# A fused memory-attention and expert kernel: sums as eight small products, a maximum in pieces, the last tile in halves, and other numbers in the planner

## The chip, the cores and the metric

The kernel runs on one core of one Trainium2 chip. The metric is the device time of one execution in microseconds. Engines go by short names: PE is TensorE (PEld its weight loads), DVE VectorE, ACT ScalarE, POOL GpSimd, SP SyncE, which issues most of the DMAs.

## The reference

Two parts follow each other. First, attention with 32 memory slots in place of 576 keys, for 8 batches and 8 heads of 64 columns:

```python
a = exp(phi - max(phi, axis=2)); a = a / (sum(a, axis=2) + 1e-9)   # over the 576 rows
k_m = einsum('bhsm,bhsd->bhmd', a, k); v_m = einsum('bhsm,bhsd->bhmd', a, v)
scores = softmax(scale * q @ k_m^T)                                # over 32 slots
x = scores @ v_m                                                   # 4608 rows of 512
```

Then a mixture of 8 experts, of which each row takes the best one:

```python
logits = x @ w_gate + modality_bias[modality_id]; e = argmax(logits)
gate = softmax(logits)[e]
out = gate * (relu(x @ w1[e]) @ w2[e])                             # 512 -> 1024 -> 512
```

## The kernel before, in words

**The work.** The kernel guesses early which expert is taken by all rows, computes with that one's weights alone and looks at the end (`bad_i`) whether the guess held. Since x is scores times v_m, the first expert product is made over the memory slots: `value_products` (L732, "vw") multiplies v_m by w1, so that a hidden tile is scores (128 slots of 4 heads, in two groups) times vw. Each big product is made of three fp32r products, high by high, low by high and high by low; the high half is a cast on ACT, the low half (`xal`, `xbl`, `vwl`, `hl`) a subtraction on DVE.

**The stages of a batch.** The maximum of phi over its rows (`mem_max`, L294 to L298: a fold of four operations on DVE; for the first batch two reductions, L306), small corrections on POOL and DVE, exp, the sums (POOL), the kv products (L403: 72 products with 32-column weights that use a quarter of the array's columns and half of its rows) and behind them one full-array product with the tile `sides` that adds the sums up over rows (L408); the turns of k_m and v_m (L148); scores ("s", L548), their softmax over slots on DVE (L593 to L625), the split of x into `xa` (part 0) and `xb` (part 1); vw twice (columns 0 to 511 and 512 to 1023, each leaving two PSUM banks that `vwl` L754 or L154 frees); the gate's small product ("vg", L528, copied by L533) and the logits ("l", L679), from which the gates come.

**The expert stages.** `hidden` (L779) makes one of 8 hidden tiles of a part: 6 products of 256 columns for part 0, 320 for part 1. ACT makes `hh` (L792) and DVE `hl` (L796) of it. `outputs` (L816) makes an output tile, 128 rows by 512 columns, in 8 steps of 3 products of 512 columns; ACT scales it by the gate (L829) and SP stores it (L837). A batch has four such tiles; a fifth (t None) takes the rest of a pair of batches. The last one of the program is that of batches 6 and 7.

**Banks.** Hidden tiles, output tiles and vw take turns in a ring of four PSUM banks ("pe"). A tile may only begin when ACT and DVE are done with the bank that is four turns back. Scores, logits, kv and vg use two other pairs of banks.

**What sets the order.** The program writes its order itself. `weave` merges two lists, the attention stages, sorted by a due time in units of expert work, and the expert stages. It keeps a model of when each engine is free, with the durations in the table `TAKES`. A stage with work for DVE is put in only if DVE's queue, by that model, is no more than a hold ahead of now: 3.5, or for the next expert stage of kind h0, h1 or h3 the number in `HOLD`. `EARLIER` moves all of a batch's due times, `AHEAD` says how far ahead of its use a batch begins. `BUSY` is the number of idle products at the start (small ones, L166, and big ones, L159); `nothing(n)` adds n more among the first stages.

## Time and profile before

| | us |
|---|---|
| median of three runs | 389.88 (389.74, 389.88, 390.06) |
| profiled execution | 389.69 |
| its span, first to last instruction | 387.9 |
| PE busy | 375.3 |
| DVE busy | 244.7 |
| ACT busy | 141.3 |
| POOL busy | 45.8 |

The span is 1.8 us shorter than the execution's time. The granted clock of TensorE is 0.994 of full speed on the mean of the span. A row of the order of time is start, duration, engine, line, operation, output<-inputs, shapes, count, and in brackets the idle time ahead with what ended it. PE records overlap: a product of 512 columns lasts 0.39 but the next starts 0.23 after it.

### The profile page before, as it was taken

The page shows a single profiled execution, that of the slowest core. Times are in us where ns is not written, and L with a number is a line of the kernel's source. Part 1 is how long each engine was busy: PE and PEld are TensorE (multiplying, and loading weights), DVE is VectorE, ACT ScalarE, POOL GpSimd, SP SyncE. Part 2 cuts the span into 40 slices and gives each one's busy share as a digit, 9 for nine tenths or more (in the row PEclk, how much of TensorE's full clock was granted, in tenths as well). Part 3 has the DMA queues.
Part 4 walks back from the last instruction along what each step waited for, and adds up shares of the span by engine and source line. Part 5 has one row for each costly group of instructions (what it writes and reads, how often), then busy time and mean ns, then how long its engine had stood idle before and what let it go on. Part 6 is the DMA issues. An engine that isn't in the chain of part 4 may idle for free.

```text
span 387.9 us, 9645 instructions
## 1 busy us (share of the span) xinstructions
PE 375.3 (97%) x3891; PEld 303.3 (78%) x3893; DVE 244.7 (63%) x613; ACT 141.3 (36%) x327; POOL 45.8 (12%) x116
## 2 busy tenths in 40 slices
PE   6899999999999999999999999999999999999993
PEld 3577976889779886788879887798868878698982
DVE  4787756895786389836786476864887467750400
ACT  2382524425234243433433334323443325241410
POOL 4347030023000400030000300003000200000000
PEclk9999999999999999999999999999999999999997
DMA  8998679875761397639712397614411011531111
GB/s 300 379 394 183 103 140 344 225 210 150 243 120 42 94 298 184 208 82 276 119 34 56 75 300 126 255 28 119 182 29 42 15 30 27 198 102 32 28 36 55
DMA packets 91307, 56.89 MB, mean 147 GB/s; under 512 B 69236, under 2 KB 74356, under 8 KB 91252
## 3 DMA queue, kind: packets, MB, share of 16 engines
q1 hardware_dynamic: 90976, 55.87, 51.4%
q8 instruction: 33, 0.54, 0.6%
q10 hardware_dynamic: 276, 0.30, 0.2%
q14 instruction: 22, 0.18, 0.2%
HBM read 37.28 MB, written 18.87 MB: 145 GB/s over the span
## 4 chain that ended last, share of the span: by engine, by line
PE 85%; DVE 4%; SPq 4%; DMA 3%; ACT 1%; issue 1%; ACTq 0%
PE pe L816 47%; PE pe L779 24%; PE pair L403 4%; PE pe L732 3%; DMA q_sb<-in_q_dram 3%; SPq L195 3%; PE pair L548 2%; PE pair L679 1%; SPq L178 1%; DVE vwl L154 1%; PE pair L148 1%; PE pair L732 1%; PE pair L408 1%; DVE xbl L662 0%; ACT ob L829 0%
## 5 line engine op out<-in xcount | busy, mean ns | idle before, releaser
L816 PE MATMUL pe<-w2h,hh 128*128 128x512 f32 x288 | 116.3, 404 | 0.0
L816 PE MATMUL pe<-w2h,hl 128*128 128x512 f32 x288 | 112.4, 390 | 0.0
L816 PE MATMUL pe<-w2l,hh 128*128 128x512 f32 x288 | 110.3, 391 | 0.0
L796 DVE SCALAR_TENSOR_TENSOR hl<-pe,hh 128x256 fp32r<-128x256 f32 (+2 forms) x158 | 58.3, 392 | 43.1 <-ACT hh L792 42.3
L816 PEld LDWEIGHTS pe<-w2h,hh 128*128 128x128 f32 x288 | 54.1, 188 | 19.8 <-issue 9.7
L792 ACT ACTIVATE hh<-pe 128x256 fp32r<-128x256 f32 (+2 forms) x158 | 53.4, 362 | 41.6 <-PE pe L779 41.2
L816 PEld LDWEIGHTS pe<-w2l,hh 128*128 128x128 f32 x288 | 54.0, 188 | 11.8
L816 PEld LDWEIGHTS pe<-w2h,hl 128*128 128x128 f32 x288 | 54.2, 188 | 9.6
L829 ACT ACTIVATE ob<-pe,gates 128x512 f32<-128x512 f32 x36 | 24.6, 687 | 73.4 <-PE pe L816 48.1
L779 PE MATMUL pe<-xbh,vwh 128*128 128x320 f32 x128 | 40.3, 315 | 0.1
L779 PE MATMUL pe<-xbh,vwl 128*128 128x320 f32 x128 | 39.6, 309 | 0.0
L779 PE MATMUL pe<-xbl,vwh 128*128 128x320 f32 x128 | 39.6, 309 | 0.0
L779 PE MATMUL pe<-xah,vwh 128*128 128x256 f32 x124 | 35.2, 287 | 1.5 <-DVE hl L796 0.7
L779 PE MATMUL pe<-xal,vwh 128*128 128x256 f32 x124 | 35.0, 284 | 0.3 <-DVE xal L662 0.3
L779 PE MATMUL pe<-xah,vwl 128*128 128x256 f32 x124 | 34.9, 283 | 0.0
L337 POOL COPY ts<-tm 32x4 f32<-32x4 f32 x24 | 4.8, 199 | 198.8 <-DVE tm L329 198.1
L779 PEld LDWEIGHTS pe<-xah,vwh 128*128 128x128 f32 x124 | 23.6, 191 | 4.2 <-ACT xah L648 1.6
L779 PEld LDWEIGHTS pe<-xbh,vwh 128*128 128x128 f32 x128 | 24.0, 188 | 1.7 <-issue 0.9
L779 PEld LDWEIGHTS pe<-xbl,vwh 128*128 128x128 f32 x128 | 24.1, 188 | 0.3
L779 PEld LDWEIGHTS pe<-xal,vwh 128*128 128x128 f32 x124 | 23.7, 191 | 0.8 <-DVE xal L662 0.5
L779 PEld LDWEIGHTS pe<-xbh,vwl 128*128 128x128 f32 x128 | 24.0, 188 | 0.0
L779 PEld LDWEIGHTS pe<-xah,vwl 128*128 128x128 f32 x124 | 23.7, 191 | 0.0
(173 smaller groups left out, 430.0 us busy)
## 6 DMA issues: line engine op xcount, KB each, us to landing
kv_sb<-in_k_dram SPq DMA_DIRECT2D x8, 1152.0 KB, 7.2
kv_sb<-in_v_dram SPq DMA_DIRECT2D x8, 1152.0 KB, 9.7
out_dram<-ob SPq DMA_DIRECT2D x64, 128.0 KB, 2.4
q_sb<-in_q_dram SPq DMA_DIRECT2D x112, 72.0 KB, 2.8
ph<-in_phi_dram SPq DMA_DIRECT2D x7, 576.0 KB, 4.3
raw<-in_moe_w_dram SPq DMA_DIRECT2D x2, 1024.0 KB, 6.4
raw<-in_moe_w_dram SPq DMA_DIRECT2D x1, 1280.0 KB, 10.2
out_dram<-ob SPq DMA_DIRECT2D x4, 256.0 KB, 2.1
```

The costliest lines, as they stand in the source:

```text
L148: nc.tensor.transpose(dst, src, ident[:rows, :rows])
L154: nc.vector.tensor_tensor(l, src, h.bitcast(F32), op=ALU.subtract)
L195: nc.sync.dma_start(*later.pop(0))
L337: nc.gpsimd.tensor_copy(ts_[BL * a:BL * (a + 1)], live["tm"][BL * o:BL * (o + 1)])
L403: nc.tensor.matmul(live["kvp"][M * j:M * (j + 1), g], lhsT=pe[half, j, c * M:(c + 1) * M], rhs=kv_sb[half, :, j, c * D:(c + 1) * D], start ...
L548: nc.tensor.matmul(sc[g][M * j:M * (j + 1), a, 0:QC * BL], lhsT=kvT[b][rows, 0, M * j:M * (j + 1)], rhs=qT[rows, j, a], start=True, stop=T ...
L732: nc.tensor.matmul(pvs[g][M * j:M * (j + 1), :], lhsT=vT[b][rows, j, :], rhs=raw1[rows, j, cols], start=True, stop=not more, tile_position ...
L779: nc.tensor.matmul(ph[:, 0:n], lhsT=(vl if k == 2 else vh)[:, g, cols], rhs=xl if k == 1 else xh, start=(g == k == 0), stop=(g == NG - 1 a ...
L792: nc.scalar.activation(hs[0][:, f, h0:h0 + p1 - p0], live["ph", f][:, p0:p1], AF.Relu)
L796: nc.vector.scalar_tensor_tensor(hl, live["ph", f][:, p0:p1], 0.0, hh.bitcast(F32), op0=ALU.max, op1=ALU.subtract)
L816: nc.tensor.matmul(po, lhsT=tile_columns(hl if n == 1 else hh, f, t), rhs=(w2l if n == 2 else w2h)[:, f, :], start=(f == n == 0), stop=(f ...
L829: nc.scalar.activation(ob, po, AF.Copy, scale=gate_of(b, t))
```

## The change

Six edits come together.

- `BUSY` goes from 92 small and 10 big idle products to 84 and 15; three `nothing` lines with 1, 4 and 3 products further on go.
- The tile `sides` and its product go. The sums are added by 8 products of 64 rows by 32 columns with a column of ones, beside each other on the array like the kv products.
- The second batch's maximum is taken by `heads_max` in three pieces (heads 0 and 1 of a partition group together, then 2, then 3), put among the first batch's stages, instead of the fold. Batches 2 to 7 keep the fold.
- The last output tile is scaled in two halves of 256 columns, one on ACT, one on DVE, and stored by two queues, SP's and ACT's.
- `HOLD` goes from 1.9, 2.4 and 2.2 to 2.2, 2.7 and 2.7.
- `EARLIER` no longer moves batch 3 (−4.0) but batch 7 (−6.0). A batch's start is its usual place minus this number, so the old value began batch 3 four later than the others, and the new one begins batch 7 six later.

```diff
--- before.py
+++ after.py
@@ -76,7 +76,7 @@
     HW = MAIN + 2 * QP
     SCALE = 1.0 / float(D) ** 0.5
     EPS = 1e-9
-    BUSY = 92, 10
+    BUSY = 84, 15
 
     FAR = float(1 << 20)
 
...
@@ -298,13 +297,16 @@
         eng.tensor_tensor(r, r, src[:, :, 8 * M:9 * M], op=op)
         return r
 
+    def heads_max(b, js):
+
+        if js.start == 0:
+            live["top", b] = wk.tile([P, HG, M], F32, name="top")
+        src = phs[b].rearrange("p j (c m) -> p j m c", m=M)
+        nc.vector.tensor_reduce(live["top", b][:, js], src[:, js], axis=AX.X, op=ALU.max)
+
     def first_max():
-
-        top = wk.tile([P, HG, M], F32, name="top")
-        src = phs[0].rearrange("p j (c m) -> p j m c", m=M)
         for js in (slice(0, HG // 2), slice(HG // 2, HG)):
-            nc.vector.tensor_reduce(top[:, js], src[:, js], axis=AX.X, op=ALU.max)
-        live["top", 0] = top
+            heads_max(0, js)
 
     def mem_max(b):
         live["top", b] = fold(nc.vector, phs[b % 2], ALU.max, "top", "top")
@@ -394,7 +396,7 @@
 
         pe, sums = live["pe", b]
         pk = pair_of_banks(1)
-        live["psum"] = pk[:, 0, 2 * D:2 * D + NG]
+        live["psum"] = pk[:, :, 2 * D]
         live["kvp"] = pk[:, :, 0:2 * D].rearrange("p g (t d) -> p g t d", t=2)
         for c in range(QC):
             for j in range(HG):
@@ -405,7 +407,13 @@
                         rhs=kv_sb[half, :, j, c * D:(c + 1) * D],
                         start=(c == 0), stop=(c == QC - 1), tile_position=(QP * g, M * j),
                     )
-        nc.tensor.matmul(live["psum"], lhsT=sums.rearrange("p j m -> p (j m)"), rhs=sides, start=True, stop=True)
+        for j in range(HG):
+            for g in range(NG):
+                half = slice(QP * g, QP * (g + 1))
+                nc.tensor.matmul(
+                    pk[M * j:M * (j + 1), g, 2 * D:2 * D + 1], lhsT=sums[half, j], rhs=ones_c[half],
+                    start=True, stop=True, tile_position=(QP * g, M * j),
+                )
 
     def first_products(t):
 
@@ -831,6 +839,15 @@
 
     def store(b, t):
         def finish(po):
+            if b == B - 1 and t is None:
+                rows = out[S * (b - 1):S * (b + 1)].rearrange("(p c) d -> c p d", c=QC)[QC - 1]
+                first, second = slice(0, DM // 2), slice(DM // 2, DM)
+                obs = [wk.tile([P, DM], F32, name="ob", bufs=2)[:, 0:DM // 2] for _ in range(2)]
+                nc.scalar.activation(obs[0], po[:, first], AF.Copy, scale=gate_of(b, t))
+                nc.vector.tensor_scalar(obs[1], po[:, second], gate_of(b, t), None, op0=ALU.mult)
+                nc.sync.dma_start(rows[:, first], obs[0])
+                nc.scalar.dma_start(rows[:, second], obs[1])
+                return
             ob = gated(b, t, po)
             if t is None:
                 rows = out[S * (b - 1):S * (b + 1)].rearrange("(p c) d -> c p d", c=QC)
@@ -862,8 +879,8 @@
...
-        "vwp": (1.15, ""), "vwpu": (1.25, "A1.1"), "vwu": (0.0, "A1.15"), "vwl": (0.0, "D1.35"),
-        "h0a": (0.24, ""), "h0b": (0.25, "A0.42 D0.45"), "k0": (2.0, ""), "kn0": (0.25, "D0.5 A0.55"), "ko0": (0.0, "D0.45"), "v0": (1.9, ""), "vn0": (0.0, "A0.5"), "kv": (2.6, "D0.4 A0.7"),
+        "vwp": (1.15, ""), "m1": (0.0, "D0.55"), "m2": (0.0, "D1.1"), "vwpu": (1.25, "A1.1"), "vwu": (0.0, "A1.15"), "vwl": (0.0, "D1.35"),
+        "h0a": (0.24, ""), "h0b": (0.25, "A0.42 D0.45"), "k0": (2.0, ""), "kn0": (0.25, "D0.5 A0.55"), "ko0": (0.0, "D0.45"), "v0": (1.9, ""), "vn0": (0.0, "A0.5"), "kv": (2.5, "D0.4 A0.7"),
...
@@ -895,7 +912,7 @@
             ("top", [("swap", b)], mem_peak, 2.0),
         ))
         for name, after, what, late in (
-            ("max", [], mem_max, 0.0),
+            *((("max", [], mem_max, 0.0),) if b > 1 else ()),
             *peaks,
             ("exp0" if b < 2 else "exp", [(peaks[-1][0], b)], mem_exp, 3.0),
             ("sums", [("exp0" if b < 2 else "exp", b)], mem_sums, 3.2),
@@ -942,9 +959,7 @@
         add(("top", 0), "top0", [("max", 0)], mem_top, 0)
         add(("preferred",), "guess", [], preferred)
         add(("guess",), "guess", [], guess)
-        nothing(1)
         add(("exp", 0), "first exp", [("top", 0)], mem_exp, 0)
-        nothing(4)
         add(("known",), "nothing", [], spread_row)
         add(("sums", 0), "first sums", [("exp", 0)], mem_sums, 0)
         add(("k", 0), "k0", [("exp", 0)], first_products, 0, floor=9.0)
@@ -986,7 +1001,6 @@
         some_hidden("hc", "h0c", [("vwl", 0, 0, 0)], range(2, 3), range(1))
         add(("vwu", 0, 1, 0), "vw1", [("vw", 0, 1)], value_upper, 1, range(1))
         add(("n", 0, 0, 1, 1), "n2", [], first_weights, 1, 1)
-        nothing(3, "pe")
         add(("xu", 0, 0, 1), "xu1", [("n", 0, 0, 1, 1)], first_split, 1, 0)
         add(("vwu", 0, 1), "vw1", [("vw", 0, 1)], value_upper, 1, range(1, 2))
         add(("w2", 0), "w2", [], first_w2, 0)
@@ -997,6 +1011,7 @@
         add(("start",), "start", [], lambda: None, floor=25.0)
         turns(1, 0, 26.5)
         turns(1, 1, 27.2)
+        add(("max", 1, 0), "m2", [], heads_max, 1, slice(0, 2), floor=26.5)
         add(("s", 0, 1), "s1", [("qt", 0, 1, 1), ("vwl", 0, 1)], first_scores, RA, RB, floor=28.6)
 
     def plan_steps(b, dues):
@@ -1049,6 +1064,11 @@
             add(("others", pair), "others", [("g", b)], others, pair)
             if b < B - 1:
                 add(("bias", pair + 1), "nothing", [], biases, pair + 1)
+        if b == 0:
+            names = [x[0] for x in todo]
+            for j, before in ((3, ("x", 0, 1)), (2, ("n", 0, 1, 0))):
+                todo.insert(names.index(before), (("max", 1, j - 1), "m1", [], heads_max, (1, slice(j, j + 1))))
+            todo += [(("max", 1), "nothing", [("max", 1, 2)], lambda: None, ())]
         for (name, kind, after, what, args), due in zip(todo, dues):
             stage(attention, name, kind, after, what, *args, due=due)
         if b == B - 1:
@@ -1113,7 +1133,7 @@
     def evenly(first, gap, n=24):
         return [first + gap * k for k in range(n)]
 
-    AHEAD, EARLIER, SPREAD = (5.8, 5.0), {3: -4.0}, 0.55
+    AHEAD, EARLIER, SPREAD = (5.8, 5.0), {7: -6.0}, 0.55
     plan_first()
     plan_steps(0, evenly(1.4, 0.25))
     plan_memory(1, 5.9, floor=27.5)
@@ -1135,7 +1155,7 @@
         at, ex = list(attention), list(experts)
 
 
-        HOLD = {"h0": 1.9, "h1": 2.4, "h3": 2.2}
+        HOLD = {"h0": 2.2, "h1": 2.7, "h3": 2.7}
 
         def ready(s):
             if not s or any(n not in done for n in s[0][2]):
...
```

The numbers set the order, so here is what is written on two engines at three places. Line numbers of the changed program are 8 or 9 higher behind L400.

DVE, batch 1, from the split of `xa` to the first hidden tiles; before:

```order
L662 TENSOR_TENSOR xal<-aT,xah 128x512
L593 STREAM_TRANSPOSE a<-pair_1084 128x320
L593 STREAM_TRANSPOSE a<-pair_1085 128x320
L754 TENSOR_TENSOR vwl<-pe,vwh 128x512 x2
L796 SCALAR_TENSOR_TENSOR hl<-pe,hh 128x256 x2
L533 COPY vg_88<-pair_1202 128x2x8
L796 SCALAR_TENSOR_TENSOR hl<-pe,hh 128x256 x2
L597 TENSOR_REDUCE mx<-a 128x20
L796 SCALAR_TENSOR_TENSOR hl<-pe,hh 128x256 x3
L599 TENSOR_TENSOR a<-a,mx 128x640
L796 SCALAR_TENSOR_TENSOR hl<-pe,hh 128x256
```

and after the change:

```order
L670 TENSOR_TENSOR xal<-aT,xah 128x512
L601 STREAM_TRANSPOSE a<-pair_1053 128x320
L601 STREAM_TRANSPOSE a<-pair_1054 128x320
L541 COPY vg_87<-pair_1170 128x2x8
L605 TENSOR_REDUCE mx<-a 128x20
L607 TENSOR_TENSOR a<-a,mx 128x640
L762 TENSOR_TENSOR vwl<-pe,vwh 128x512 x2
L804 SCALAR_TENSOR_TENSOR hl<-pe,hh 128x256 x6
```

The copy of vg, the maximum and the subtraction of the second scores (`mx`, `a`) now stand ahead of `vwl`, which stood ahead of them.

PE, batch 5, the logits and the vw product among output steps; before:

```order
L816 MATMUL pe<-w2h,hh 128x512
L816 MATMUL pe<-w2h,hl 128x512
L816 MATMUL pe<-w2l,hh 128x512
L679 MATMUL pair_3367<-aT,vg_90 32x128 x8
L679 MATMUL pair_3367<-aT,vg_90 32x32 x8
L732 MATMUL pe<-raw_106,kvT_85 32x512 x8
L816 MATMUL pe<-w2h,hh 128x512
L816 MATMUL pe<-w2h,hl 128x512
```

and now:

```order
L687 MATMUL pair_3372<-aT,vg_89 32x128 x8
L687 MATMUL pair_3372<-aT,vg_89 32x32 x8
L824 MATMUL pe<-w2h,hh 128x512
L824 MATMUL pe<-w2h,hl 128x512
L824 MATMUL pe<-w2l,hh 128x512
L824 MATMUL pe<-w2h,hh 128x512
L824 MATMUL pe<-w2h,hl 128x512
L824 MATMUL pe<-w2l,hh 128x512
L824 MATMUL pe<-w2h,hh 128x512
L824 MATMUL pe<-w2h,hl 128x512
L824 MATMUL pe<-w2l,hh 128x512
L740 MATMUL pe<-raw_105,kvT_84 32x512 x8
```

The two sets of small products followed each other; now nine products of 512 columns lie between them.

DVE, from the second scores of batch 3 to the first `hl` of the next hidden tiles, with the logits (`lgT`, `lg`), the gates (`gates`, `badp`) and batch 4's maximum (`t2top`, `top`). Before, both pairs of `vwl` stood ahead of the logits, and from the gates on the rows were:

```order
L706 TENSOR_REDUCE se<-ex 128x5
L707 TENSOR_SCALAR se<-se 128x5
L708 RECIPROCAL gates<-se 128x5
L713 TENSOR_SCALAR other<-fms,known 128x9
L714 TENSOR_REDUCE badp<-other 128x1
L294 TENSOR_TENSOR t2top<-ph_104 128x512
L295 TENSOR_TENSOR t2top<-t2top 128x4x64
L297 TENSOR_TENSOR top<-t2top 128x128
L298 TENSOR_TENSOR top<-top,ph_104 128x128
L796 SCALAR_TENSOR_TENSOR hl<-pe,hh 128x256 x4
```

Now one pair of `vwl` stands ahead of the logits and one behind the gates:

```order
L715 TENSOR_SCALAR se<-se 128x5
L716 RECIPROCAL gates<-se 128x5
L721 TENSOR_SCALAR other<-fms,known 128x9
L722 TENSOR_REDUCE badp<-other 128x1
L153 TENSOR_TENSOR vwl<-pe,vwh 128x512 x2
L293 TENSOR_TENSOR t2top<-ph_103 128x512
L294 TENSOR_TENSOR t2top<-t2top 128x4x64
L296 TENSOR_TENSOR top<-t2top 128x128
L297 TENSOR_TENSOR top<-top,ph_103 128x128
L804 SCALAR_TENSOR_TENSOR hl<-pe,hh 128x256
L329 STREAM_TRANSPOSE tt<-top 128x128
L331 TENSOR_REDUCE tm<-tt 128x4
```

The logits and gates have moved ahead of the second vw's remainder, and the maximum stays behind it, still ahead of `hl`.

4 lines of the change are left out of this document (removed).

## The prediction

> **What bounds the kernel now.** I read the page first, then a table of busy time by stretches, then the order of time around each gap.
>
> ```profile
> PE 375.3 (97%) x3891; PEld 303.3 (78%) x3893; DVE 244.7 (63%) x613; ACT 141.3 (36%) x327; POOL 45.8 (12%) x116
> PE 85%; DVE 4%; SPq 4%; DMA 3%; ACT 1%; issue 1%; ACTq 0%
> ```
>
> The first row is busy time by engine, the second the chain that ended last: TensorE (PE) is 97% busy and 85% of the chain. The table by stretches says where the missing 3% is.
>
> ```profile
> sum 25.00, PE 20.53 PEld 12.82 DVE 16.96 ACT 10.59 POOL 7.85; mean PE 4.11 PEld 2.56 DVE 3.39 ACT 2.12 POOL 1.57
> ...
> core 0: us, PE busy (x) PEld busy (x) DVE busy (x) ACT busy (x) POOL busy (x), PEclk, DMA share, GB/s
> ...
> 60.00:70.00 10.00, 9.21 (x92) 6.02 (x77) 8.22 (x17) 4.37 (x8) 0.00 (x0) 1.00 1.00 327
> ...
> 160.00:165.00 5.00, 4.26 (x36) 4.05 (x35) 4.72 (x17) 2.49 (x7) 0.29 (x2) 1.00 0.57 192
> 165.00:380.00 215.00, 215.00 (x1999) 176.71 (x1999) 124.79 (x315) 74.65 (x177) 15.25 (x34) 1.00 0.36 100
> ```
>
> PE idles 4.47 us before 25 us, then 0.79 us in the stretch from 60 to 70 and 0.74 in the one from 160 to 165. Between 165 and 380 there is no gap at all. The other stretches up to 380 are as full, and behind 380 PE has little left to do: the last tile leaves. So after 25 us an edit can pay in three ways: fill those two gaps, shorten what PE itself does, or shorten the tail. Work moved on another engine pays nothing unless PE waits for it.
>
> **The change, part by part.** The sum is made against the profiled execution, 389.69 us, which is 0.19 under the median 389.88.
>
> *Start.* Five big idle products that stood behind the first maximum move ahead of it; three at about 22 us go, with eight small ones and four memsets.
>
> ```profile
> 3.12 2.60 PE L159 MATMUL pair<-busy 128*128 128x512 bf16 x8 [0.22 <-issue]
> 6.77 0.30 PE L148 MATMUL pair<-ident,top 128*128 128x128 f32 x1 [1.05 <-DVE top L306]
> ```
>
> Eight idle products take 2.60 us and PE then waits 1.05 us for the maximum. Five more at the warm pace (half of the mean 0.33 at least, so 0.8 to 1.1 us) fill that wait; the three at 22 us stand ahead of a tile whose split ScalarE delivers later, so PE waits there with or without them. I take 0, with −0.1 to +0.3 as bounds.
>
> *The second batch's maximum.* A fold of four operations (1.6 us) goes and three pieces come.
>
> ```profile
> L306 DVE TENSOR_REDUCE top<-ph 128x64 f32<-128x576 f32 x2 | 2.2, 1118 | 4.5 <-DMA ph<-in_phi_dram 4.5
> 31.15 0.91 DVE L593 STREAM_TRANSPOSE a<-pair 128x320 f32<-128x320 f32 x2 [1.85 <-PE pair L566]
> ```
>
> The big piece costs 1.12 us and the two small ones half of that each, an estimate from the same row: 2.24 together. VectorE's idle 1.85 here takes the big one, and later gaps of the same chain, in which VectorE waits for ScalarE, the small ones. PE waits for VectorE at none of these places: 0. Without the later gaps the overhang is 2.24 − 1.85 = 0.4 of VectorE's time, and that is the bound.
>
> *Near 68 us, batch 1's first hidden tiles.* PE waited 0.46 + 0.34 = 0.80 for the split of xa; now the steps of batch 1 come earlier and the split is ready, so 0.80 is saved. But the order on VectorE at this place is a new one.
>
> ```profile
> 67.65 0.39 PE L779 MATMUL pe<-xah,vwh 128*128 128x256 f32 x1 [0.46 <-ACT xah L659]
> 68.38 0.39 PE L779 MATMUL pe<-xal,vwh 128*128 128x256 f32 x1 [0.34 <-DVE xal L662]
> ...
> 69.88 0.26 PE L528 MATMUL pair<-wgd,kvT 128*32 128x16 f32 x8
> 70.06 0.39 PE L779 MATMUL pe<-xah,vwh 128*128 128x256 f32 x1
> ...
> 298.63 5.75 PE pe L779 x48
> ...
> 69.07 1.25 DVE L754 TENSOR_TENSOR vwl<-pe,vwh 128x512 fp32r<-128x512 f32 x2
> ...
> 70.91 0.16 DVE L533 COPY vg<-pair 128x16 f32<-128x16 f32 x1
> 72.62 0.81 DVE L597 TENSOR_REDUCE mx<-a 128x20 f32<-128x640 f32 x1
> ```
>
> Before, vwl (the remainder that frees the two PSUM banks of vw) ran first, and the copy of vg, mx and the subtraction came after it, between the hl. Now vg's products stand right behind vw's, and the queue is copy, mx, subtraction, vwl. Let S be the start of vg's products on PE. They end at S+0.26, the copy at S+0.4, mx and the subtraction over the same 128x640, 0.81 each, at S+2.0, and the first half of vwl at S+2.7, when its bank is free. On PE vg takes 0.18 (69.88 to 70.06), then two tiles of six products at 0.12 each (48 in 5.75, the row of the chain), with 0.1 more at the first: PE asks for the third bank at S+1.7. It waits 1.0 us, where before it did not. Net +0.20; the bounds are −0.80 (no wait at all) and +0.6 (a second wait like it, 0.4).
>
> *Near 163 us, batch 4's first hidden tiles.*
>
> ```profile
> 160.88 0.68 DVE L294 TENSOR_TENSOR t2top<-ph 128x512 f32<-128x512 f32 x1
> ...
> 162.59 1.41 DVE L796 SCALAR_TENSOR_TENSOR hl<-pe,hh 128x256 fp32r<-128x256 f32 x4
> ...
> 163.06 0.39 PE L779 MATMUL pe<-xah,vwh 128*128 128x256 f32 x1 [0.74 <-DVE hl L796]
> ```
>
> Logits, gates and batch 4's maximum stood in one row ahead of hl, and PE waited 0.74 for the bank that hl frees. Logits and gates now come before the second vw product, six output steps earlier, so behind vwl (1.3) only the maximum (1.7, 160.88 to 162.59) is left ahead of hl. Both end before the ring is full again. I take −0.74; the other bound is 0.
>
> *Batch 3's chain four us earlier, batch 7's six us later.* Batch 3's maximum now also stands ahead of hl, of which PE needs the first one only four tiles later: 0, with little to spare. For batch 7 I have the present slack:
>
> ```profile
> 342.29 0.42 DVE L796 SCALAR_TENSOR_TENSOR hl<-pe,hh 128x256 fp32r<-128x256 f32 x1 [0.67 <-ACT hh L792]
> ```
>
> VectorE is done 0.67 us before the first hl. The later chain uses up most of this; I take 0, with 0 to +0.5 (a chain one microsecond too long for the slack would leave 0.3 to 0.5 of it on PE); beyond that it is case D below.
>
> *The eight small products.* Seven times (batches 1 to 7) one full-array product, two passes, becomes eight small ones, 16 passes.
>
> ```profile
> 365.13 16.34 PE pe L816 x72
> ...
> 173.77 0.30 PEld L408 LDWEIGHTS pair<-sides,sums 128*128 128x128 f32 x2 [0.20 <-issue]
> ...
> 174.02 0.48 PE L816 MATMUL pe<-w2h,hh 128*128 128x512 f32 x1
> 174.33 0.40 PE L816 MATMUL pe<-w2h,hl 128*128 128x512 f32 x1
> ...
> 11.51 0.29 PE L433 MATMUL pair<-ones_c,sums 64*64 64x1 f32 x8
> 11.65 2.07 PE L422 MATMUL pe<-kv_sb,exp 64*64 64x128 f32 x68
> ...
> L528 PE MATMUL pair<-wgd,kvT 128*32 128x16 f32 x64 | 2.0, 193 | 0.0
> ```
>
> Before: the weight load waits 0.20 for the small products to leave, 0.25 passes to the next big product, and the second big one comes 0.31 later instead of 0.23 (72 of them in 16.34 in the chain): 0.53 in all. After: eight small passes of L528 last 0.26 with 0.193 for the last, so they start (0.26−0.19)/7 = 10 ns apart; 15 such steps are 0.15, going in is about 0.05, and a visit of small products costs 0.21 on its way out (the last of the eight at 69.88 starts at 69.95, the next big product at 70.06, and another 0.10 is lost ahead of the one behind, as at 198.90 below). That makes 0.41, a gain of 0.12 each, 0.85 for seven. By the slowest reading of L433, 0.14 over eight passes or 17.5 ns, the eight products cost 0.53 and the gain is nothing; bounds −1.0 to 0.
>
> The Trainium skill, "TensorE: Matmul & The Clock Gate", section "Wait — 56ns, not 53.3ns?", says that matmuls never start less than about 25 ns apart however small they are; sixteen passes would then take 0.38 and the seven places would cost 0.8 more than before. The row of L433 disagrees: its eight passes, on different parts of the array, are 17.5 ns apart or less.
>
> *Visits that are no longer joined.* The higher holds on VectorE move small products on PE too: vw and logits of a batch, which ran one behind the other, are now split by output steps.
>
> ```profile
> 197.56 0.39 PE L816 MATMUL pe<-w2l,hh 128*128 128x512 f32 x1
> 197.88 1.09 PE L732 MATMUL pe<-raw,kvT 64*32 64x512 f32 x16
> 198.90 0.50 PE L816 MATMUL pe<-w2h,hh 128*128 128x512 f32 x1
> 199.24 0.39 PE L816 MATMUL pe<-w2h,hl 128*128 128x512 f32 x1
> ...
> 246.01 0.77 PE L679 MATMUL pair<-aT,vg 128*32 128x128 f32 x32
> 246.71 1.09 PE L732 MATMUL pe<-raw,kvT 64*32 64x512 f32 x16
> 247.73 0.50 PE L816 MATMUL pe<-w2h,hh 128*128 128x512 f32 x1
> ```
>
> A visit of small products costs (0.32−0.23) + (0.34−0.23) = 0.20 at its two borders, beside the 1.02 of its own; joined, the 0.70 of the logits and the 1.02 follow each other with no border. Nine pairs were joined before: vg with vw four times, logits with vw three times, scores with vw twice. Three are now, all of vg with vw. So six borders are new: four of the kinds quoted, 4 × 0.20 = 0.80, and the two with scores, which the trace shows only joined, for which I take +0.10 together out of −0.2 to +0.4. That is +0.90, with +0.6 to +1.2.
>
> *Tail.*
>
> ```profile
> L792 ACT ACTIVATE hh<-pe 128x256 fp32r<-128x256 f32 x94 | 36.1, 385 | 29.6 <-PE pe L779 29.3
> ...
> 381.54 0.69 ACT L829 ACTIVATE ob<-pe,gates 128x512 f32<-128x512 f32 x1 [4.75 <-PE pe L816]
> ...
> 0.73 0.48 ACTq L1204 DMA_DIRECT2D ph<-in_phi_dram  x1
> ```
>
> A half takes ScalarE 0.39 instead of 0.69: −0.30; VectorE's half runs beside it. The second transfer is issued by ScalarE's own queue, 0.48 for an issue, after VectorE's half; SP issued the whole one before. For that I charge 0.10 and take −0.20. The bounds are −0.35 (half the bytes in each transfer land a little sooner) and +0.1 (most of the 0.48 stands on the path).
>
> **Sum:** 0 + 0 + 0.20 − 0.74 + 0 − 0.85 + 0.90 − 0.20 = −0.69. The profiled execution comes to 389.0 and the median to 389.88 − 0.69 = 389.2.
>
> **Rivals.** *B, the prices that I charge don't fall due:* either the 1.0 us wait at batch 1 isn't there, because what VectorE does ahead of vwl is ready early, or borders cost less. For it: in the trace the vg copy, mx and the subtraction were spread among hl without delaying PE. Against it: the queue on VectorE runs in the written order. Either one gives 389.2 − 1.0 = 388.2.
>
> *C, the sums bring nothing:* the 17.5 ns above; 389.2 + 0.85 = 390.0. The full-array product is then no worse than eight small ones. For it speaks that L433's passes are the only ones with one column; against it L528's 10 ns. Should the passes be dearer still, as products that follow each other on the same part of the array might, it would be C2: 0.11 lost at each place and not won, 389.2 + 0.85 + 0.8 = 390.85. (The page's rule above is this case.)
>
> *D, slower:* batch 7's chain, six us later, ends too late. Its place lies in the stretch from 165 to 380, where PE has no gap today. PE would wait there first for the split of xa, as at 67.65 and 68.38, and then for the bank, as at 163.06: 0.80 + 0.74 = 1.54. It decides once the chain is more than the 0.67 of VectorE's slack too late. 389.2 + 1.5 = 390.7.
>
> *E, the clock:* where idle products are taken away, PE could be granted half its clock again. The eight at 3.12 took 2.60 where the warm pace of 512 columns, 0.23, gives 1.82, so the end of a cold stretch cost 0.78; a whole one may cost twice that, 1.6: 390.8. Against it: five idle products are added in front, and the three at 22 us that go are less than a microsecond among hidden tiles.
>
> **How the numbers follow.** What a measurement of this kernel can tell from no change is about 0.2%, 0.78 us: faster is under 389.10, slower is over 390.66. The likeliest case, A, the sum as it stands, gets 0.53, with a range of its own from 388.6 to 389.8 (half of the wait, half of the borders, half of the sums to either side). B gets 0.27, because two of the larger terms are charges that I read from an order and not from a trace; C 0.06 and C2 0.01, since L433's row speaks against the latter; D 0.09; E 0.04. Faster: all of B and 0.23 of A, 0.50. Same: the other 0.30 of A and C, 0.36. Slower: C2, D and E, 0.14. The range leaves out the slower cases and the lowest part of B, 0.06: 387.9 to 390.4.
>
> **What would show it right or wrong.** Right: near 163 the row with 0.74 is gone; at 68 the two waits for the split are gone, and a wait of about 1.0 us for vwl stands at the third hidden tile of batch 1; L816 follows the last kv product after about 0.3 instead of 0.45; small-product visits are 52 in place of 46, each with a first gap of 0.32; the last activation takes about 0.4. Wrong: a wait at batch 1 that is missing or twice as long, PE busy under 214.5 us in the last 215 before the tail (D), a granted clock under 1.00 before 30 us (E), or a first product behind the sums that is no earlier than 0.45 (C).

## The result, and the profile after

The changed kernel takes 392.02 us (four runs, 391.87 to 392.33) against 389.81 (four runs, 389.54 to 390.06): the ratio is 1.0053, with a 95% interval of 1.0039 to 1.0067. It is slower by 0.53%. The forecast was 389.2.

The profiled execution takes 391.98, with a span of 389.8, against 389.69 and 387.9. Of the 2.29 us, 1.9 lie in the span and 0.4 outside it (2.18 against 1.79). From the page of the changed kernel, busy time by engine and the chain that ended last:

```profile
PE 376.1 (96%) x3979; PEld 301.8 (77%) x3980; DVE 245.8 (63%) x613; ACT 141.0 (36%) x327; POOL 46.0 (12%) x112
PE 95%; DVE 2%; issue 1%; ACT 1%; POOL 0%; ACTq 0%; DVEq 0%; POOLq 0%
```

PE is busy for 0.8 us more than before. Busy time by stretches, PE's number behind the stretch's length, the granted clock third from the end:

```profile
15.00:20.00 5.00, 3.71 (x92) 1.49 (x90) 3.28 (x11) 2.54 (x7) 2.74 (x12) 1.00 1.04 360
20.00:25.00 5.00, 4.11 (x39) 2.07 (x40) 3.48 (x10) 3.05 (x7) 0.60 (x1) 1.00 1.07 382
...
60.00:70.00 10.00, 10.00 (x74) 6.49 (x75) 7.58 (x17) 4.18 (x8) 0.00 (x0) 1.00 1.00 351
70.00:80.00 10.00, 9.04 (x62) 8.26 (x61) 8.62 (x19) 4.49 (x11) 0.00 (x0) 1.00 0.94 232
...
160.00:165.00 5.00, 5.00 (x36) 4.62 (x35) 4.24 (x11) 2.18 (x5) 0.46 (x3) 1.00 0.48 163
165.00:382.00 217.00, 217.00 (x2072) 178.50 (x2071) 125.66 (x318) 75.47 (x179) 15.08 (x33) 1.00 0.36 99
```

The gap near 163 us is closed, the one near 68 has become one near 72, batch 7's later chain has opened none, and the clock is 1.00. What is new lies ahead of 25 us: 1.29 and 0.89 us of idle PE in the two stretches from 15 to 25, where the kernel before has 0.39 and 0.31. The order of time on PE there:

```profile
3.05 4.09 PE L158 MATMUL pair<-busy 128*128 128x512 bf16 x13 [0.22 <-issue]
7.00 0.30 PE L147 MATMUL pair<-ident,top 128*128 128x128 f32 x1
...
9.37 2.19 PE L430 MATMUL pair<-kv_sb,exp 64*64 64x128 f32 x72 [0.62 <-ACT exp L373]
11.74 0.29 PE L441 MATMUL pair<-ones_c,sums 64*64 64x1 f32 x8 [0.18 <-DVE sums L387]
11.88 1.28 PE L430 MATMUL pe<-kv_sb,exp 64*64 64x128 f32 x35
13.79 1.31 PE L430 MATMUL pe<-kv_sb,exp 64*64 64x128 f32 x37 [0.63 <-issue]
15.03 0.44 PE L147 MATMUL pair<-ident,keys 128*128 128x128 f32 x2
15.93 1.07 PE L574 MATMUL pair<-q_sb,kT 32*32 32x128 f32 x64 [0.46 <-ACT kT L526]
16.93 0.33 PE L147 MATMUL pe<-ident,values 128*128 128x128 f32 x1
17.61 1.09 PE L740 MATMUL pair<-raw,kvT 64*32 64x512 f32 x16 [0.35 <-ACT kvT L531]
18.50 1.03 PE L740 MATMUL pe<-raw,kvT 64*32 64x512 f32 x7
20.89 1.07 PE L740 MATMUL pe<-raw,kvT 64*32 64x512 f32 x9 [1.36 <-issue]
```

In the kernel before, the same two sets of products run through:

```profile
11.65 2.17 PE L422 MATMUL pe<-kv_sb,exp 64*64 64x128 f32 x72
17.61 1.11 PE L732 MATMUL pe<-raw,kvT 64*32 64x512 f32 x16
```

Two waits of the changed kernel, 0.63 and 1.36, end on "issue": the profile shows no engine, buffer or load that released them. Both stand in the middle of one line's products, where the program says nothing about waiting. Between them lie 37 + 2 + 64 + 1 + 16 + 7 = 127 products, each with its weight load.

The starts of ACT's operation on each output tile (ob) say how the loss adds up. The first tile of the program comes 1.91 later than before (44.26 against 42.35), the last one 1.50 later (383.04 against 381.54). So between these two profiled executions the start costs 1.91, everything between saves 0.41, the tail costs 0.4 in the span and 0.4 more outside it: 1.91 − 0.41 + 0.4 + 0.4 = 2.3.

### The profile page after: what moved, and what is told of

Same layout as the page of the kernel before. It is cut to its first block, busy times and chain, and to the rows that moved or that the text cites. A ratio compares the mean times of both kernels' runs of the same rounds, so it can differ in the third digit from the quotient of the medians.

```text
span 389.8 us, 9834 instructions
## 1 busy us (share of the span) xinstructions
PE 376.1 (96%) x3979; PEld 301.8 (77%) x3980; DVE 245.8 (63%) x613; ACT 141.0 (36%) x327; POOL 46.0 (12%) x112
## 4 chain that ended last, share of the span: by engine, by line
PE 95%; DVE 2%; issue 1%; ACT 1%; POOL 0%; ACTq 0%; DVEq 0%; POOLq 0%
PE pe L824 52%; PE pe L787 26%; PE pe L740 4%; PE pair L405 4%; PE pair L556 2%; PE pair L687 1%; PE pair L158 1%; PE pe L430 1%; PE pair L147 1%; PE pair L574 1%; PE pair L740 1%; PE pair L536 0%; PE pair L787 0%; PE pair L413 0%; ACT exp L373 0%
## 5 line engine op out<-in xcount | busy, mean ns | idle before, releaser
L152 ACT CAST vwh<-pe 128x512 fp32r<-128x512 f32 x26 | 14.0, 590 | 29.6 <-PE pe L740 29.6
## 6 DMA issues: line engine op xcount, KB each, us to landing
raw<-in_moe_w_dram SPq DMA_DIRECT2D x1, 1280.0 KB, 10.2
```

The costliest lines, as they stand in the source:

```text
L152: nc.scalar.copy(h, src)
```

## The experiments

### The start: the idle products also move the code

First the kernel before with eight fewer small idle products, and nothing else:

```diff
-    BUSY = 92, 10
+    BUSY = 84, 10
```

> The kernel before with 84 small idle products instead of 92, nothing else. Theory 1: the same two waits turn up in the kernel before: 391.3 to 391.9 against 389.8. Theories 2 and 3: 389.8, no change.

It took 391.64 (391.39 to 392.05) against 389.93, ratio 1.0039 (1.0027 to 1.0050). Its PE rows:

```profile
11.76 1.28 PE L422 MATMUL pe<-kv_sb,exp 64*64 64x128 f32 x35
13.37 1.31 PE L422 MATMUL pe<-kv_sb,exp 64*64 64x128 f32 x37 [0.32 <-issue]
...
18.07 1.03 PE L732 MATMUL pe<-raw,kvT 64*32 64x512 f32 x7
20.09 1.06 PE L732 MATMUL pe<-raw,kvT 64*32 64x512 f32 x9 [0.99 <-issue]
```

The two waits stand behind the same 35 and 7 products as in the changed kernel, and its tiles come 1.76 later at the first and 1.81 at the last. Fewer idle products alone make nearly all of the start's loss. The granted clock is 1.00 there, and the 72 kv products ahead of the first wait take 2.20 as against 2.19 in the kernel before, so it isn't the clock.

What ends such a wait is seen in the DMA view. On its instruction queue, q8, the page counts over the execution:

```profile
q8 instruction: 33, 0.54, 0.6%
```

That is 33 packets of 16 KB. In the changed kernel one of them runs from 11.28 for 1.15 us and one from 18.43 for 1.13. PE goes on 1.36 and 1.33 us after they end, at 13.79 and 20.89. I then counted PE's records (products, weight loads, its own waits) from the start of the execution: the two waits stand at numbers 448 and 704, 256 apart. All 23 such waits in the traces of 13 kernels, near 13, 18, 20, 94, 96 and 175 to 179 us, stand at a number that leaves 191 to 193 when divided by 256. So PE's program arrives in blocks of 256 instructions, and PE stands still at a border between two blocks when the next one isn't there. PE's records in this trace are 8080, which is 32 blocks. The Trainium skill, "Trainium Architecture — The Big Picture", section "The software stack", says that an instruction has 64 bytes; 256 of them are the 16 KB of a packet, which agrees.

Then the changed kernel with more idle products, so that the early block comes in time:

```diff
-    BUSY = 84, 15
+    BUSY = 92, 15     (in the second run 88, 15)
```

> The changed kernel with 92 small idle products at the start instead of 84; the 15 big ones and all else stay. Theory 1 (code): the changed kernel loses 1.9 us before 25 us in two waits of TensorE that no semaphore ends (0.63 in the 36th of 72 kv products, 1.36 in the 8th of 16 vw products), 254 matmuls and weight loads apart; TensorE's code comes in blocks, a block is asked for when an earlier one is used up, and with eight small products fewer that point falls behind eight or so big idle products. With 92 both waits go: 390.1 (389.6 to 390.5). Theory 2 (loads): the first loads come later because of other traffic at the start; eight small products change nothing in that: 392.0. Theory 3 (idle products): the three that went at 22 us are missed: 392.0.

> The same with 88 small idle products. Theory 1: the border of the block moves by four big idle products of 0.2 to 0.4 us, so the code is asked for about 1 us earlier than with 84: the first wait (0.63) goes, the second gets shorter: 390.3 to 391.3, between 84 and 92. Theories 2 and 3: 392.0.

They took 393.12 (392.36 to 393.93; ratio 1.0074, 1.0048 to 1.0100) and 392.25 (391.35 to 395.45; 1.0063, 1.0037 to 1.0089). The waits at the start are gone, and the first tile is 0.90 and 0.76 late instead of 1.91. But waits of the same kind came up elsewhere, here with 92:

```profile
94.26 0.41 PE L787 MATMUL pe<-xbh,vwh 128*128 128x320 f32 x1 [0.46 <-issue]
...
175.80 0.22 PE L413 MATMUL pair<-ones_c,sums 64*32 64x1 f32 x2 [1.25 <-issue]
```

Sixteen instructions more at the start move every later border by 16. My expectation had the start right and missed that.

A third try had as many idle products as the changed kernel, 99, but eight more of them small; the expectation put the border at the 94th product:

```diff
-    BUSY = 84, 15
+    BUSY = 92, 7
```

> The changed kernel with 92 small and 7 big idle products instead of 84 and 15: as many instructions ahead of the first real product as in the change, so that every later instruction keeps its place in its code block, but the first border (by theory 1 the 94th product) comes at the second big product instead of the tenth, some 2.5 us earlier, and PE is free when the maximum comes. Theory 1 (code in blocks): both waits at the start go and none turns up near 175: 1.9 us less than the change, 390.1 (389.7 to 390.6). Rival (clock): with half the big idle products the clock falls at the start, 0.8 to 1.6 us lost: 391 to 392. Rival (loads): 392.0.

392.28 (391.89 to 392.71; 1.0060, 1.0042 to 1.0078). The code still came late (packet at 11.37), and the rival held as well, PE was slow when the first kv products came:

```profile
9.80 3.76 PE L430 MATMUL pair<-kv_sb,exp 64*64 64x128 f32 x72 [0.64 <-ACT exp L373]
```

The same 72 products take 2.19 in the two main kernels. That this is the clock is read from the pace and from where the trace's record of the granted clock begins, with 1.00: at 13.1 us here, at 5.3 in the changed kernel. When the code comes goes, in all runs, by how many idle products stand ahead of the wait for the first maximum, small or big: with 102 or more the first packet starts at 5.9 to 6.8, with 99 or fewer at 11.1 to 11.4. The kernel before has 102, the changed one 99. Between the two nothing was tried.

At last the changed kernel with the whole start of the kernel before:

```diff
-    BUSY = 84, 15
+    BUSY = 92, 10
...
+        nothing(1)
...
+        nothing(4)
...
+        nothing(3, "pe")
```

> The changed kernel with the start of the kernel before (92 small and 10 big idle products, and the 1, 4 and 3 further on). Code theory, now with numbers: in all runs so far, TensorE's waits without a releaser stand at its 192nd instruction or a multiple of 256 behind it (448, 704, 2496, 4288), and a block is asked for early only if more than 200 instructions lie ahead of the wait for the first maximum. Here both hold early again: the start's 1.9 us go. But every later instruction moves 22 places, so that the border at 4288 falls into the end of the kv visit of batch 4 near 174 us: a wait of 1.2 to 1.5 there, and perhaps 0.1 to 0.5 near 93. 392.0 - 1.9 + 1.6 = 391.7 (391.3 to 392.0). Rival (the start alone is the loss): 390.1.

393.93 (393.07 to 396.44; 1.0087, 1.0067 to 1.0107). Borders fall late in two kv visits again, and PE waits 2.46 near 95.7 and 1.38 near 179.4. The places were expected and the second size too; the first wait is far over the 0.1 to 0.5 that was expected. The profiled execution was the longest of the six, 396.44, and in it the granted clock is also at 0.50 from 97.0 to 100.4 us, so its sizes are not those of the median. And the first tile is still 0.79 late, with no wait on issue ahead of it.

### The rest of the start: eight bytes in front of the tiles

In that kernel the load of q_sb lands 0.7 us later than in the kernel before: DVE's transpose of it starts at 13.48 instead of 12.74. The change takes the tile `sides` away, and its four memsets on POOL. Two runs test this, one that takes them from the kernel before (with the eight small products, so that nothing reads the tile), and one that gives them back to the kernel above; the edit of the first, which the second turns round:

```diff
-    sides = const.tile([P, NG], F32, name="sides")
...
-        for g in range(NG):
-            for e in range(NG):
-                nc.gpsimd.memset(sides[QP * g:QP * (g + 1), e:e + 1], float(g == e))
```

> The kernel before with eight small products in all seven batches (as run already), and without the four memsets of the sides tile on POOL, which nothing reads any more. Question: in the kernels built from the changed one, whose code arrives early, the load of q_sb lands about 0.7 us later (13.5 instead of 12.7). Theory (the memsets missing at the start shift POOL or the loads): the transpose of q_sb starts at 13.4 to 13.6 here too. Rival (something else in the changed code, memory placement for one): it starts at 12.6 to 12.8.

> The changed kernel with the start of the kernel before (as run already), and with the four memsets put back. Theory (memsets): the transpose of q_sb starts at 12.6 to 12.8 instead of 13.48, and the first output tile comes 0.7 us earlier than without them. Rival (something else): 13.4 to 13.6, as without them. Waits on issue at the kv visits of batches 2 and 4 as before (1 to 2.5).

Two more took tile and memsets apart: the tile alone, never used, and four memsets of the same shape without it, written into `places`.

> The changed kernel with the start of the kernel before, and with the tile sides allocated again (8 bytes a partition, ahead of all later tiles) but never written or read. Theory (placement: the 8 bytes shift every tile behind it in SBUF, and the loads of the start land faster at the one place than at the other): the transpose of q_sb starts at 12.6 to 12.8, as with tile and memsets together (12.76). Theory (the memsets themselves): 13.4 to 13.6, as without either (13.48).

> The same kernel without the tile, but with four memsets of the same shape at the same place on POOL, written into the tile places (whose own memsets overwrite them). Theory (placement): the transpose of q_sb starts at 13.4 to 13.6. Theory (the memsets, by the time that they take on POOL): 12.6 to 12.8.

The transposes on DVE, in the kernel before without tile and memsets, and in the changed one with the old start and with both, with the tile alone, and with the memsets alone:

```profile
13.40 0.71 DVE L544 STREAM_TRANSPOSE q_sb<-q_sb 128x512 f32<-128x512 f32 x1 [0.55 <-DMA q_sb<-in_q_dram]
```

```profile
12.76 0.71 DVE L548 STREAM_TRANSPOSE q_sb<-q_sb 128x512 f32<-128x512 f32 x1 [0.33 <-DMA q_sb<-in_q_dram]
```

```profile
12.68 0.71 DVE L548 STREAM_TRANSPOSE q_sb<-q_sb 128x512 f32<-128x512 f32 x1 [0.20 <-DMA q_sb<-in_q_dram]
```

```profile
13.64 0.71 DVE L547 STREAM_TRANSPOSE q_sb<-q_sb 128x512 f32<-128x512 f32 x1 [1.22 <-DMA q_sb<-in_q_dram]
```

The tile decides, the memsets do nothing. The first output tile of the changed kernel with the old start follows: +0.06 with both, −0.06 with the tile alone, +0.79 with neither, +1.04 with the memsets alone. In the first of the four it is 1.93 late, and only part of that is the load:

```profile
18.00:20.00 2.00, 2.00 (x31) 0.61 (x17) 1.86 (x7) 0.60 (x2) 1.74 (x7) 0.50 1.04 388
```

The granted clock was 0.50 here (in the trace from 17.6 to 21.0), and a packet came at 16.14 instead of 14.81; together they cost PE about 1.3 us among the vw products. Each of the four kernels ran once (392.98, 392.23, 392.72 and 393.13 us, with waits on issue of 1.5 to 2.0 near 175 and 177), but the seven versions without the tile and with early code have the load 11.1 to 11.3 us after its issue where the view gives it, those with the tile 9.7 to 10.5. In the changed kernel itself, without the tile but with late code, it is 10.1, and 10.0 to 10.2 in three more like it. So the missing tile costs nothing there; it shows once the code comes early, and then takes some 0.8 of the 1.9 that the repairs of the start could win. Why the two go together, these runs don't say.

The tile has 8 bytes a partition and stands ahead of the tiles that are loaded, so it moves their addresses. No run here shows the addresses, and the changed kernel's 10.1 speaks against them as the whole reason.

### Eight small products: the sums alone

```diff
-        nc.tensor.matmul(live["psum"], lhsT=sums.rearrange("p j m -> p (j m)"), rhs=sides, start=True, stop=True)
+        for j in range(HG):
+            for g in range(NG):
+                half = slice(QP * g, QP * (g + 1))
+                nc.tensor.matmul(
+                    pk[M * j:M * (j + 1), g, 2 * D:2 * D + 1], lhsT=sums[half, j], rhs=ones_c[half],
+                    start=True, stop=True, tile_position=(QP * g, M * j),
+                )
```

First in all seven batches of the kernel before:

> The kernel before with only the eight small products in place of the full-array one, its order unchanged. In the traces of before and of the change the kv visit with its sums takes 2.60 and 2.41, so theory: 7 x 0.19 = 1.3 less, 388.6, and 'den' no later. Rival by the code theory: each kv visit now holds 28 instructions more, so the borders of the blocks fall elsewhere, and one wait of 0.5 to 1.2 comes in: 389.1 to 389.8. Rival: the wait of PE for something else takes the gain: 389.9.

391.02 (390.57 to 391.85), ratio 1.0030 (1.0019 to 1.0040): slower, though each visit is shorter. PE waits 0.29 on issue near 94 and 1.47 near 175, inside the sums themselves, and 0.55 near 17.8, where the code is the same as before and the packet came at 15.31 instead of 14.81. A visit with 72 kv products runs through some 290 instructions in about two microseconds (each product is two passes with a weight load each). A fetch takes longer: in the changed kernel 2.5 us from the start of a packet to the next instruction. A visit that crosses a border early and reaches the next one while still small runs dry. Big products, 0.23 us each, give the fetch time.

That gave a test in which the arithmetic is the same and only the borders move. From the records of the kernel before I worked out where they fall for each choice of four batches, with the new sums there and the old ones elsewhere:

```diff
...
+        if b in (3, 4, 5, 6):     # in the second run (2, 4, 6, 7)
+            for j in range(HG):
...
+            return
         nc.tensor.matmul(live["psum"], lhsT=sums.rearrange("p j m -> p (j m)"), rhs=sides, start=True, stop=True)
```

> The kernel before, with one edit: batches 3, 4, 5 and 6 take their sums as eight small products, batches 1, 2 and 7 keep the one full-array product. Theory (code in blocks of 256 PE instructions): each of the four changed visits saves 0.19 us (as 2.60 to 2.41 between the two kernels), 0.76 in all, and moves every later block border by 28 instructions. Counted in the instruction stream of the kernel before, no border then falls in the last part of a kv visit: no wait on issue at any kv visit behind 25 us, and the median comes out 0.5 to 0.8 us below the kernel before. Rival (sixteen small passes, or what surrounds them, cost as much as the full-array product): no change, 0 to +0.3. Rival (a kv visit with eight small products stalls wherever it stands): four stalls of up to 1.5, +2 or more.

> The same edit in the same number of batches, but in 2, 4, 6 and 7. Theory (blocks of 256): the same four savings, 0.76, but the borders now fall late in the kv visits near 94 us, 267 us and 313 us: waits on issue of about 1.1 (0.9 to 1.2), 0.75 (0.6 to 0.9) and 0.2, 2.0 in all, so that the median is 1.0 to 1.5 us above the kernel before, and some 2.0 above the kernel with the edit in batches 3 to 6. Rival (it is the number of small passes that counts, not where they stand): both kernels take the same time.

With batches 3 to 6: **388.99 us** (388.80 to 389.51, 11 runs) against 389.97 for the kernel before, run beside it: ratio 0.9978, with a 95% interval of 0.9969 to 0.9987. This version beats both kernels. With batches 2, 4, 6 and 7: 390.24 (389.65 to 390.57), 1.0008 (0.9999 to 1.0018). That is no different from the kernel before, where 1.0 to 1.5 more was expected. But the two versions differ by 1.25 us, so the place decides; the rival of equal times is out. In the first kernel's trace PE waits on issue nowhere behind 10 us, and a sum with the next big products reads:

```profile
173.46 0.29 PE L412 MATMUL pair<-ones_c,sums 64*32 64x1 f32 x16
173.69 0.50 PE L825 MATMUL pe<-w2h,hh 128*128 128x512 f32 x1
174.02 0.39 PE L825 MATMUL pe<-w2h,hl 128*128 128x512 f32 x1
```

Its tiles gain 0.19 at each of the four visits; the last comes 0.67 earlier. In the second kernel batch 2's visit pays:

```profile
93.81 0.29 PE L412 MATMUL pair<-ones_c,sums 64*32 64x1 f32 x16
94.03 0.42 PE L788 MATMUL pe<-xbh,vwh 128*128 128x320 f32 x1
94.29 0.31 PE L788 MATMUL pe<-xbl,vwh 128*128 128x320 f32 x1
95.46 0.31 PE L788 MATMUL pe<-xbh,vwl 128*128 128x320 f32 x1 [0.85 <-issue]
```

I had expected 1.1 there, 0.75 near 267 and 0.2 near 313. The first came as 0.85, the third as 0.27 (the product at 313.50 starts 0.50 behind the one before it, not 0.23), the second not at all. My time for a fetch, 3.2 us from one border to the use of the next block, held at both waits (92.29 to 95.46 and 310.23 to 313.50). It isn't a constant, though: near 267 the packet started at 260.72, 4.6 us before PE reached the border at 265.34 among big products, and so it was early.

Two attempts at a faster whole failed. Both have the old start and tail, `EARLIER` empty and four sums of 64 by 64 instead of eight of 64 by 32; the first has h1 at 2.4, the second the holds of the change and `BUSY = 101, 10`:

```diff
-        for j in range(HG):
+        for j in range(0, HG, 2):
...
-                    pk[M * j:M * (j + 1), g, 2 * D:2 * D + 1], lhsT=sums[half, j], rhs=ones_c[half],
+                    pk[M * j:M * (j + 2), g, 2 * D:2 * D + 1], lhsT=sums[half, j:j + 2].rearrange("p j m -> p (j m)"),
...
```

> A version meant to beat both: the start and the tail of the kernel before, the maximum in pieces, batches 3 and 7 both at their usual start, the hold h1 at 2.4, and the sums as four small products of 64 by 64 (8 passes) instead of eight. By the positions counted, no kv visit has a code border in its last part. Terms: sums -7 x 0.2 = -1.4; batch 4's wait -0.74; three visits more than before, +0.6; batch 1's wait for the split stays: 389.9 - 1.5 = 388.4 (387.9 to 389.0). Rival (a code border or a VectorE wait that I have not seen): 389.5 to 390.5.

> The same with the holds of the change (2.2, 2.7, 2.7) and 101 small idle products, which put the code borders outside the kv visits for its order. Against the version with h1 at 2.4: three visits more (+0.6), batch 1's wait of 0.96 for vwl in place of 0.80 for the split (+0.16): 389.1 (388.6 to 389.7).

391.41 (390.39 to 392.23; 1.0031, 1.0019 to 1.0042) and 392.01 (391.49 to 394.38; 1.0062, 1.0034 to 1.0089). Neither waits for code at a kv visit. But both start 0.7 late (neither has the tile), the first also waits 0.53 at 60 us for kvT and again for the split of xa, and four sums of twice the width gain nothing: the first one's kv visits with their sums take 2.60, as with the full-array product, and from batch 4 on its lateness stays at 1.3.

### The order alone

The kernel before with only the maximum in pieces, `HOLD`, `EARLIER` and the planner's costs; sums, start and tail as before, with the idle products at 99 and 10:

```diff
-    AHEAD, EARLIER, SPREAD = (5.8, 5.0), {3: -4.0}, 0.55
+    AHEAD, EARLIER, SPREAD = (5.8, 5.0), {7: -6.0}, 0.55
...
-        HOLD = {"h0": 1.9, "h1": 2.4, "h3": 2.2}
+        HOLD = {"h0": 2.2, "h1": 2.7, "h3": 2.7}
```

> The kernel before with the order of the change alone: pieces of the second batch's maximum, the new holds and starts of batches 3 and 7; the full-array sums, the old start and the old tail stay. 99 small idle products instead of 92 put the code borders of all seven kv visits outside the visits. The terms of the prediction for the order, with what the trace of the change showed: -0.80 + 0.96 at batch 1, -0.74 at batch 4, +1.15 for the visits no longer joined: +0.6, 390.4 (390.0 to 390.8). Rival (the order gains, the visits cost nothing): 389.3.

390.48 (390.33 to 391.24), 1.0015 (1.0005 to 1.0025). The last tile comes 0.75 later and no wait on issue is seen. The steps for the order gave 0.20 − 0.74 + 0.90 = +0.36, or +1.0 with the wait at 0.16 and the borders at 1.6, as the trace after has them (below). The expectation had +0.6 with 1.15 for the borders, which is five of the six. This part of the change costs time by itself, and the run agrees with that.

The wait near 72 us alone, taken back by h1 at 2.4 in a kernel with 92 and 7 idle products and the last tile in one piece, with a kernel beside it that has only these two:

```diff
-        HOLD = {"h0": 2.2, "h1": 2.7, "h3": 2.7}
+        HOLD = {"h0": 2.2, "h1": 2.4, "h3": 2.7}
```

> The same again with the hold h1 at its old 2.4: the copy of vg, mx and the subtraction of batch 1 come behind vwl again, between the hl. Theory (the queue on VectorE holds the bank): the wait of 0.96 us for vwl at the third hidden tile of batch 1 goes: 389.6 - 1.0 = 388.6, if the wait for the split of xa (0.80) doesn't come back; with it 389.4. By the code theory a shift of later instructions can also cost up to 1.2.

> The same with the last tile in one piece on ScalarE. If start and tail are apart from each other, the gains add up: 390.1 - 0.5 = 389.6, about the time of the kernel before.

391.13 (390.81 to 391.42; 1.0031, 1.0021 to 1.0042) and 391.80 (391.01 to 392.26; 1.0044, 1.0031 to 1.0057). With h1 at 2.4 the wait for vwl (0.96) is gone and the two for the split (0.49 and 0.34) are back. Between the first and the last tile this kernel gains 0.81 on the kernel before, the one beside it 0.52: h1 at 2.7 costs 0.3. Both stay above what was expected of them, since they have the late code and the slow kv products of the run with 92 and 7. Of the other 0.4 between the medians the traces don't tell much: the first tiles come 1.69 and 2.21 late, but the second profiled execution was granted half the clock from 8.2 to 15.0 us.

### The tail

The changed kernel with its last tile in one piece:

```diff
-            if b == B - 1 and t is None:
+            if False:
```

> The changed kernel with the last tile scaled by ScalarE in one piece and stored by one transfer, as before. In the trace of the change VectorE's half begins only when ScalarE's half ends, and the second transfer is issued 0.3 us later behind the last product than the one before; so theory 1: 0.3 to 0.5 faster than the change, 391.6. Rival: the halves gain the 0.2 that was predicted, and the missing time is elsewhere: 392.2.

391.22 (391.02 to 391.84), 1.0034 (1.0021 to 1.0047), 0.8 less than the changed kernel had. In the profiled execution some 0.3 of that is a start whose waits happened to be shorter (0.34 and 1.23), which leaves some 0.5 for the tail. The last rows of the order of time, before and in the changed kernel, are:

```profile
381.06 0.39 PE L816 MATMUL pe<-w2l,hh 128*128 128x512 f32 x1
382.25 0.35 SPq L837 DMA_DIRECT2D out_dram<-ob  x1
```

```profile
382.57 0.39 PE L824 MATMUL pe<-w2l,hh 128*128 128x512 f32 x1
383.04 0.47 ACT L846 ACTIVATE ob<-pe,gates 128x256 f32<-128x256 f32 x1 [4.75 <-PE pe L824]
383.54 0.35 SPq L848 DMA_DIRECT2D out_dram<-ob  x1
383.55 0.48 DVE L847 TENSOR_SCALAR ob<-pe,gates 128x256 f32<-128x256 f32 x1 [15.76 <-ACT ob L846]
384.06 0.38 ACTq L849 DMA_DIRECT2D out_dram<-ob  x1
```

DVE's half waits for ACT's, 383.55 behind 383.04 + 0.47: the two halves read the same PSUM tile, and run one after the other. The row names ACT's operation as what released DVE; why the one had to wait for the other was not tested. A half takes 0.47, not 0.39. So the second transfer is issued 1.49 after the start of the last product, against 1.19 for the one transfer before. And eight profiled executions with the tile in halves took 2.12 to 2.24 us outside their span, the twelve with it in one piece 1.74 to 1.87. That is the other 0.4; why the end of an execution takes longer, the trace doesn't show. The 0.4 within the span is less certain: from the start of the last product to the span's end it is 7.24 in the changed kernel and 6.84 before, but 6.9 to 7.2 in the eight and 6.6 to 7.6 in the twelve.

## Why the prediction was wrong

**The direction was wrong, by two of its terms.** The step that failed first is *Start*: "I take 0, with −0.1 to +0.3 as bounds". It costed the idle products as time on PE and as warmth for its clock, and neither lost anything (the clock is 1.00 behind 5.3 us). It didn't see that they are also instructions. With three fewer of them ahead of the first maximum a block of code comes almost 5 us later, and two borders then cost 0.63 + 1.36 on PE: +1.91 at the first tile. No rival held this.

*Tail* had the wrong sign: −0.20 predicted, with +0.1 as the upper bound; +0.8 between the two profiles, some +0.5 by the run that takes it back. "VectorE's half runs beside it" is the sentence that fell: it runs behind it. The half's 0.39 came from hidden tiles' ACT rows, and was 0.47; the time outside the span was not looked at.

**The rest was close, partly by luck**: −0.41 measured between the first and the last tile, −0.49 predicted (0.20 − 0.74 − 0.85 + 0.90). Two of its terms, the sums and the borders, were off by 0.5 and 0.7 to opposite sides.

- *Batch 1*: the wait for vwl, worked out from the order on VectorE as 1.0, is there:

```profile
70.85 0.28 PE L787 MATMUL pe<-xah,vwl 128*128 128x256 f32 x1
72.08 0.36 PE L787 MATMUL pe<-xah,vwh 128*128 128x256 f32 x1 [0.96 <-DVE vwl L762]
```

  It stands at the third hidden tile, as written, and the 0.80 for the split is gone: +0.16 for +0.20. Rival B's first half fell with it.
- *Near 163*: the 0.74 is gone. Batch 7's slack held: no gap between 165 and 382. D did not happen. E did not either, though the 92 and 7 products show that it was near.
- *Eight small products*: a gain, and larger than taken. Where I had 0.12 each, the visits have 0.19:

```profile
174.59 0.29 PE L413 MATMUL pair<-ones_c,sums 64*32 64x1 f32 x16
174.82 0.50 PE L824 MATMUL pe<-w2h,hh 128*128 128x512 f32 x1
175.15 0.39 PE L824 MATMUL pe<-w2h,hl 128*128 128x512 f32 x1
```

  Sixteen passes and the way to the next big product take 0.23 (174.59 to 174.82), 14 ns a pass or less. With 25 ns a pass, as the Trainium skill's "TensorE: Matmul & The Clock Gate" has it (section "Wait — 56ns, not 53.3ns?"), the passes alone would take 0.38; the trace disagrees again, and C and C2 are out as prices of PE. As a result C came true in another way: alone, in all seven batches, the sums lost time, through the code.
- *Borders*: 52 visits for 46, as counted, but they cost 1.6 for 0.90, above the range of 0.6 to 1.2. A visit's cost is taken here from the last big product ahead of it to the second one behind it, less the pace of big products. The four borders with logits and vg cost 0.8, as priced: logits and vw took 1.92 in one visit and take 0.90 + 1.22 in two. The two with scores, for which I had +0.10 together, cost 0.8 as well: batch 2's took 2.19 with vw and take 1.33 + 1.22, batch 1's 2.81 and now 2.04 + 1.22:

```profile
58.09 1.91 PE L556 MATMUL pair<-q_sb,kvT 64*32 64x288 f32 x32
59.93 0.50 PE L824 MATMUL pe<-w2h,hh 128*128 128x512 f32 x1
```

  Batch 1's scores take 0.7 longer than the later ones. That isn't late code: PE's records have the numbers 1634 to 1704 here, and the next border is at 1728. Six of PE's own waits stand among these products, some 0.12 apart, in the kernel before too; what they wait for was not followed up. Then 0.16 − 0.74 − 1.3 + 1.6 = −0.3, near the −0.41.

## What to carry to other kernels

Where PE runs through instructions faster than they can be fetched (here 290 small ones in two microseconds, against some 3.2 from one border to the use of the next block), a wait on "issue" in the middle of one line's products is late code: count the instructions between two such waits, and look at the instruction queue's packets. An edit then pays or not by where it moves the borders, so try it at several places before it is judged: the same edit in four batches made the kernel 0.22% faster, or with another choice of four not faster at all. Where a tile goes, look at the loads into the tiles behind it. Where work is split over two engines, look in the trace whether the halves run beside each other; here they didn't. And look at the granted clock of the stretch before a loss is put down to anything else: two traces here have 3.4 us at half the clock, another 6.8.

## What the hardware showed that I had not expected

PE's code comes in packets of 16 KB for 256 instructions; the 23 waits for code in 13 kernels all stand at one place in the block, numbers 191 to 193. PE goes on 1.3 to 1.5 us after the packet ends.

Eight bytes a partition ahead of the loaded tiles moved the end of a load of 512 KB, seen at the transpose that waits for it, by 0.7 to 1.0 us, in kernels whose code comes early.

ACT and DVE, each with one half of a PSUM tile, ran one after the other, 0.47 and 0.48; whether the chip or the program's own order makes the second wait is open. Storing the last tile by two queues instead of one left 0.4 us more outside the span, in all 8 profiles with it and in none of the 12 without.

Left open: a version of the changed kernel with the tile allocated, its last tile in one piece and the new sums only where borders allow it was not tried.
